# Attention weights divided on one engine: a fused attention and gated-MLP kernel on one core

## The chip, the cores and the metric

One core of a Trainium2 chip. The metric is device time in microseconds (us) of one execution, lower is better. The engines are named as in the profile: PE (TensorE), DVE (VectorE), ACT (ScalarE), POOL (GpSimd), SP (SyncE, which issues most DMAs).

## The reference

Three stages in float32 on batch 2, sequence 768:

```python
# 1. attention, 8 heads of 64; a key is kept if it is one of the first 8, or at most 95 back
scores = q @ k.T / 8 - slope[h] * dist        # NEG where not kept
a = exp(scores - max); a = a / (sum(a) + 1e-9)
x = a @ v                                     # heads side by side: (2, 768, 512)
# 2. gated value:  x = (sigmoid(causal conv5(x)) * (x @ w_val)) @ w_out
# 3. gated MLP:    h = relu(x @ w_in)         # 512 -> 1024
#                  out = (h * sigmoid(conv3(h))) @ w_out2   # 1024 -> 512
```

The weights come as float64 and are brought to float32 in the kernel.

## The kernel before, in words

*Attention.* `fast_attention` runs over 12 tiles of 128 queries (6 per batch). A tile sees its own 128 keys and the 128 of the tile before (the first 32 places of which are replaced by the global keys where needed, `first_keys`, L511), so it is 128x256 per head, 128x128 in the first tile of a batch. Per tile, in two halves of four heads: score products on PE (L461) into PSUM; on DVE bias and row minimum (L472, writes the tile `p`); on ACT the exponential in place with its row sum (L477); on POOL a guard of 1e-9 on the four sums (L488); on DVE their reciprocal (L491); then the **division**: each head's `p` is multiplied in place by its reciprocal, on DVE (L498) or on POOL (L501). PE transposes two heads at a time into one PSUM bank (L528); ACT or DVE copies them to `pts` (L532, L538); PE makes the output products (L553), and ACT or DVE copies the tile into `x` (L570, L576). There are 11 buffers for `p` and one PSUM bank for the transposes.

*Weights.* Each 128x512 unit of a float64 matrix comes by DMA as two words per value and passes ACT (L262), POOL (L264), and DVE twice (L269, L272); most are then split into a high and a low part (L234 on ACT, L236 on DVE) for three-term products (`mm3`, L243 to L245). `w_out @ w_in` is multiplied out first (L319).

*The rest.* Convolutions are chains of DVE steps (L671) opened on ACT or POOL (L666, L667); then values, hidden layer and projection for four chunks of the sequence.

*The order.* Every piece of work is handed to a `Plan` with its engine and an assumed duration. A piece may have several **ways** (engines): the planner picks the engine on which it would end first. It lays all work out by list scheduling in six passes, keeps the layout that ends first by its assumed durations, and issues every engine's instructions in that fixed order. Weight work has an earlier rank (`EARLY`). Before the change a division had two ways, with these assumed durations for `nk` keys:

```python
pl.add(
    "DVE", 0.13 + 0.00052 * nk, on_dve, [p[h], st], [("r", t, half)], [("p", t, h)],
    POOL=(0.1 + pool_us(nk), on_pool),          # pool_us(n) = 0.17 + 0.0013 * n
)
```

For 256 keys that is 0.263 us on DVE and 0.603 on POOL. The copies L532/L538 and L570/L576 have two ways as well, ACT and DVE.

Of the kernel before, what the change touches and what calls it, by code (L numbers as in the profile page):

```python
# [36 lines left out]
BIG = NEG * 2.0 ** NH * 1.01  # L37
QKSCALE = 1.0 / math.sqrt(D)
XPAIRS = 2
RAWS, MBUFS, HBUFS, Z2BUFS, PBUFS, PTBUFS, KQBUFS, VBUFS = 3, 2, 6, 3, 11, 4, 3, 4  # L40
EARLY = -5.0
LANDING = 2.4
# [40 lines left out]
class Plan:  # L83

    LAG = {"PE": 0.2, "ACT": 0.15, "DVE": 0.15, "POOL": 0.15, "SP": 0.0}
    START = {"DVE": 0.4, "ACT": 1.2, "SP": 0.3}
# [134 lines left out]
def pool_us(n):  # L223
    return 0.17 + 0.0013 * n
# [27 lines left out]
def to_f32(c, dst, raw, n, bufs, reads, token):  # L252
# [5 lines left out]
    def whole(): return high().bitcast(F32)  # L258
    def bits(): return dst().bitcast(I32)
# [3 lines left out]
    pl.add(  # L263
        "POOL", pool_us(n), lambda: nc.gpsimd.tensor_scalar(whole(), whole(), 0.0, 1.0, ALU.mult, ALU.mult),  # L264
        bufs, reads + [token], [tail],
# [143 lines left out]
def fast_attention(c, ap):  # L409

    nc, ident, pl = c.nc, c.ident, c.plan
# [29 lines left out]
    def held(d, ts):  # L441
        return [d[t] for t in ts if t in d]

    for t in range(nt):
        b, i = tiles[t]
        if t and i == 0:
            yield
        js = [t - 1, t] if i else [t]
        nk = len(js) * P
        st, p = sts.new(), {}  # L450
        load(t)
        for half in range(2):
            s = [c.ring["s"].new() for z in range(2)]

            def scores(half=half, s=s, js=js, t0=t):
                for pr in (2 * half, 2 * half + 1):
                    for n, j in enumerate(js):
                        for z in range(2):
                            hs = slice(z * D, (z + 1) * D)
                            out = s[z].t.rearrange("p (a w) -> p a w", w=WIN)[:, pr % 2, n * P : (n + 1) * P]  # L460
                            nc.tensor.matmul(out, keys(t0, pr, 1)[hs], keys(j, pr, 0)[hs], start=True, stop=True)  # L461

            pl.add(
                "PE", 0.43 * len(js), scores, s + held(kq, js), [("kq", j) for j in js], [("s", t, half)], mode="s"
            )
            for h in range(4 * half, 4 * half + 4):
                p[h] = pr_.new()

                def least(h=h, s=s, st=st, w=p[h], nk=nk, i=i):
                    sc = s[h % 2].t.rearrange("p (a w) -> p a w", w=WIN)[:, h // 2 % 2, :nk]  # L470
                    bias = c.B[:, h, :] if i else c.B0[h]
                    nc.vector.tensor_tensor_reduce(  # L472
                        w.t[:, :nk], sc, bias, -QKSCALE, 3.0e38, ALU.add, ALU.min, st.t[:, 0, h : h + 1]
                    )

                def grow(h=h, st=st, w=p[h], nk=nk):
                    nc.scalar.activation(  # L477
                        w.t[:, :nk], w.t[:, :nk], AF.Exp, bias=st.t[:, 0, h : h + 1], scale=-1.0,
                        accum_out=st.t[:, 1, h : h + 1],
                    )  # L480

                bias = ("B" if i else "B0", h)
                pl.add("DVE", dve_us(nk), least, [p[h], s[h % 2], st], [("s", t, half), bias], [("p", t, h)])
                pl.add("ACT", act_us(nk, True, True, True), grow, [p[h], st], [], [("p", t, h)])
            hs = slice(4 * half, 4 * half + 4)

            def guard(st=st, hs=hs):
                nc.gpsimd.tensor_scalar(st.t[:, 1, hs], st.t[:, 1, hs], 1.0e-9, 1.0, ALU.add, ALU.mult)  # L488

            def invert(st=st, hs=hs):  # L490
                nc.vector.reciprocal(st.t[:, 2, hs], st.t[:, 1, hs])  # L491

            four = [("p", t, h) for h in range(4 * half, 4 * half + 4)]
            pl.add("POOL", 0.12, guard, [st], four, [("r", t, half)])
            pl.add("DVE", 0.2, invert, [st], [], [("r", t, half)])
            for h in range(4 * half, 4 * half + 4):
                def on_dve(h=h, st=st, w=p[h], nk=nk):
                    nc.vector.tensor_scalar(w.t[:, :nk], w.t[:, :nk], st.t[:, 2, h : h + 1], None, ALU.mult)  # L498

                def on_pool(h=h, st=st, w=p[h], nk=nk):  # L500
                    nc.gpsimd.tensor_scalar(w.t[:, :nk], w.t[:, :nk], st.t[:, 2, h : h + 1], 1.0, ALU.mult, ALU.mult)  # L501

                pl.add(
                    "DVE", 0.13 + 0.00052 * nk, on_dve, [p[h], st], [("r", t, half)], [("p", t, h)],
                    POOL=(0.1 + pool_us(nk), on_pool),
                )

        def first_keys(t=t, i=i):
            r = (c.first[0] if t == 0 else kq[t].t)[:, :, 0, 0:GW]
            a, z = (gl, r) if i == 0 else (r, gl)  # L510
            nc.gpsimd.tensor_scalar(a, z, 1.0, 1.0, ALU.mult, ALU.mult)  # L511

        if i == 0:
            pl.add("POOL", 0.4, first_keys, held(kq, [t]), [("kq", t)], ["gl"])
        elif i < NT - 1:
            pl.add("POOL", 0.4, first_keys, held(kq, [t]), ["gl"], [("kq", t)])

        xp = c.ring["x"].new()
        pts = {}
        for pr in range(NPAIR):  # L520
            pt = c.ring["t"].new()
            pts[pr] = ptr.new()

            def turn(pr=pr, pt=pt, p=p, nw=len(js)):
                o = pt.t.rearrange("p (z n q) -> p z n q", z=2, n=2)
                for z in range(2):
                    for n in range(nw):
                        nc.tensor.transpose(o[:, z, n, :], p[2 * pr + z].t[:, n * P : (n + 1) * P], ident)  # L528

            def copy(pt=pt, w=pts[pr], nw=len(js)):  # L530
                o = pt.t.rearrange("p (z n q) -> p z n q", z=2, n=2)
                nc.scalar.activation(w.t[:, :, :nw, :], o[:, :, :nw, :], AF.Copy)  # L532

            two = [p[2 * pr], p[2 * pr + 1]]
            pl.add("PE", 0.218 * len(js), turn, [pt] + two, [("p", t, 2 * pr), ("p", t, 2 * pr + 1)], [("pt", t, pr)])
            def by_dve(pt=pt, w=pts[pr], nw=len(js)):
                o = pt.t.rearrange("p (z n q) -> p z n q", z=2, n=2)
                nc.vector.tensor_copy(w.t[:, :, :nw, :], o[:, :, :nw, :])  # L538

            pl.add(  # L540
                "ACT", act_us(2 * nk, False), copy, [pt, pts[pr]], [("pt", t, pr)], [("pts", t, pr)],
                DVE=(dve_us(2 * nk), by_dve),
            )

            if pr % XPAIRS < XPAIRS - 1:
                continue

            def output(prs=range(pr - XPAIRS + 1, pr + 1), pts=pts, xp=xp, js=js):
                o = xp.t.rearrange("p (a q) -> p a q", q=P)
                for pr in prs:  # L550
                    for n, j in enumerate(js):
                        for z in range(2):
                            nc.tensor.matmul(  # L553
                                o[z * D : (z + 1) * D, pr, :], vals(j, 2 * pr + z), pts[pr].t[:, z, n, :],
                                start=n == 0, stop=n == len(js) - 1,
                            )

            prs = range(pr - XPAIRS + 1, pr + 1)
            pl.add(
                "PE", 0.213 * len(js) * XPAIRS, output, [xp] + [pts[q] for q in prs] + held(vs, js),  # L560
                [("pts", t, q) for q in prs] + [("v", j) for j in js], [("xp", t, q) for q in prs], mode="x",
            )
        if 0 < i < NT - 1:
            pl.add(
                "SP", dma_us(64), lambda b=b, t=t: nc.sync.dma_start(vs[t].t[0:GW], c.v[b, 0:GW].rearrange("s (a h) d -> s a h d", a=2)),
                [vs[t]], [], [("v", t)], delay=LANDING,
            )
        pl.add(
            "ACT", act_us(512, False),
            lambda xp=xp, i=i: nc.scalar.activation(  # L570
                c.x[:, :, XP + i * P : XP + (i + 1) * P], xp.t.rearrange("p (a q) -> p a q", q=P), AF.Copy
            ),
            [xp], [("xp", t, pr) for pr in range(NPAIR)], [("x", i)] + (["d", "d0"] if t in (0, 1, 4) else []),
            DVE=(
                dve_us(512),
                lambda xp=xp, i=i: nc.vector.tensor_copy(  # L576
                    c.x[:, :, XP + i * P : XP + (i + 1) * P], xp.t.rearrange("p (a q) -> p a q", q=P)
                ),
            ),
        )  # L580
# [420 lines left out]
```

## Time and profile before

| | before |
|---|---|
| median of 3 runs | 289.19 us (288.85 to 289.6) |
| profiled execution | 289.12 us |
| its span (first to last instruction) | 286.9 us |
| PE, DVE, ACT, POOL busy | 270.1, 238.6, 187.2, 95.4 us |
| granted PE clock | 0.998 of full speed |
| divisions on DVE, on POOL | 46, 50 |

The time of a run is the span and some 2 us around it. A row of instructions is read as: line of the kernel, engine, operation, tile written <- tiles read, shapes and count; after the bar the busy time of the group, the mean in ns of one, and the idle time of the engine just before them with what ended it. PE's matmuls are pipelined and their ends are modelled, so a busy PE is not one at its peak. A row of windows has the stretch, its length, the busy time of each engine with the instructions that start in it, the granted clock, the share of the DMA engines and GB/s.

### The profile page before, as it was taken

To read this page: it belongs to the slowest core of one execution; us is meant where nothing else is said; L and a number is where in the kernel's file an instruction comes from. 1 tells how busy PE (TensorE), PEld (TensorE's weight loads), DVE (VectorE), ACT (ScalarE), POOL (GpSimd) and SP (SyncE) were. 2 spreads that over 40 slices of the span, in tenths; PEclk is the share of its full clock that TensorE was granted. 3 is DMA by queue.
4 is the path that set the end of the run, shared out by engine and by line. 5 is a ranking of instruction groups with operands and counts; after the bars stand their busy time and mean duration, and the time that the engine had idled before them with its cause. 6 is when DMAs were issued, how large, how long until landed. Compare 5 with 4: busy or idle time off the path is not lost.

```text
span 286.9 us, 5416 instructions
## 1 busy us (share of the span) xinstructions
PE 270.1 (94%) x1832; PEld 227.9 (79%) x1832; DVE 238.6 (83%) x607; ACT 187.2 (65%) x468; POOL 95.4 (33%) x208
## 2 busy tenths in 40 slices
PE   2689799999999999999999999999999999999993
PEld 2567556564557998999999999988999988899882
DVE  3899999999999999999899999999985654356600
ACT  2899798967677879775688554894464354445510
POOL 4555557445554405563443310320512000003000
PEclk9999999999999999999999999999999999999999
DMA  4985756645634111023510000010000011000112
GB/s 133 344 322 143 239 197 213 251 138 169 216 108 148 48 65 58 9 75 93 170 43 0 2 0 0 1 39 38 37 2 0 0 73 39 37 0 2 39 73 85
DMA packets 10276, 26.17 MB, mean 91 GB/s; under 512 B 1408, under 2 KB 2688, under 8 KB 10240
## 3 DMA queue, kind: packets, MB, share of 16 engines
q1 hardware_dynamic: 9440, 25.22, 26.3%
q10 hardware_dynamic: 800, 0.52, 0.6%
q8 instruction: 16, 0.26, 0.4%
q14 instruction: 20, 0.16, 0.2%
HBM read 22.59 MB, written 3.15 MB: 90 GB/s over the span
## 4 chain that ended last, share of the span: by engine, by line
PE 73%; DVE 15%; POOL 3%; issue 3%; ACT 3%; POOLq 1%; DVEq 0%; ACTq 0%
PE s L244 8%; PE s L245 8%; PE s L243 8%; PE f L243 7%; PE f L245 7%; PE f L244 7%; PE s L461 4%; PE x L553 4%; PE t L528 4%; DVE p L472 3%; DVE z L671 2%; PE t L243 2%; PE t L245 2%; PE x L245 2%; PE x L244 2%
## 5 line engine op out<-in xcount | busy, mean ns | idle before, releaser
L477 ACT ACTIVATE p<-p,st 128x256 f32<-128x256 f32 (+1 forms) x96 | 46.1, 483 | 8.0 <-DVE st L472 6.4
L671 DVE SCALAR_TENSOR_TENSOR z<-h,cw,z 128x384 f32<-128x384 f32 x64 | 39.9, 630 | 12.6 <-ACT z L666 10.9
L673 ACT ACTIVATE z<-z 128x384 f32<-128x384 f32 (+2 forms) x48 | 25.2, 524 | 26.2 <-DVE z L671 25.5
L671 DVE SCALAR_TENSOR_TENSOR z<-x,cw,z 128x400 f32<-128x400 f32 (+1 forms) x64 | 39.6, 643 | 0.2
L244 PE MATMUL s<-w,g 128*128 128x512 f32 (+1 forms) x104 | 39.2, 377 | 0.0
L245 PE MATMUL s<-w,g 128*128 128x512 f32 (+1 forms) x104 | 39.2, 377 | 0.0
L243 PE MATMUL s<-w,g 128*128 128x512 f32 (+1 forms) x104 | 39.1, 376 | 0.0
L501 POOL TENSOR_SCALAR p<-p,st 128x256 f32<-128x256 f32 (+1 forms) x50 | 32.5, 660 | 11.0 <-DVE st L491 8.7
L528 PEld LDWEIGHTS t<-ident,p 128*128 128x128 f32 x176 | 19.8, 141 | 16.6 <-issue 5.0
L528 PE MATMUL t<-ident,p 128*128 128x128 f32 x176 | 28.7, 282 | 4.1 <-ACT pts L532 2.1
L319 PE MATMUL f<-w,w 128*128 128x512 f32 x64 | 30.8, 602 | 0.0
L472 DVE CUSTOM_DVE_ANT_0 p<-s,B 128x256 f32<-128x256 f32 x80 | 30.5, 410 | 0.0
L243 PE MATMUL f<-gg,Wh 128*128 128x400 f32 (+1 forms) x80 | 27.7, 347 | 0.0
L245 PE MATMUL f<-gg,Wl 128*128 128x400 f32 (+1 forms) x80 | 27.0, 338 | 0.0
L244 PE MATMUL f<-gg,Wh 128*128 128x400 f32 (+1 forms) x80 | 27.0, 338 | 0.0
L461 PE MATMUL s<-kq 64*128 64x128 f32 x320 | 25.7, 292 | 0.8 <-DVE st L472 0.7
L461 PEld LDWEIGHTS s<-kq 64*128 64x128 f32 x320 | 21.5, 194 | 4.9 <-issue 2.6
L667 POOL TENSOR_SCALAR z<-h,cw 128x384 f32<-128x384 f32 x10 | 8.9, 887 | 45.9 <-DVE z L671 31.0
L264 POOL TENSOR_SCALAR raw<-raw 128x512 f32<-128x512 f32 x24 | 18.3, 764 | 16.7 <-ACT m L262 14.1
L236 DVE TENSOR_TENSOR g<-z,g 128x384 fp32r<-128x384 f32 x32 | 17.8, 562 | 5.9 <-ACT g L234 5.9
L245 PEld LDWEIGHTS s<-w,g 128*128 128x128 f32 x104 | 19.5, 188 | 3.8
L244 PEld LDWEIGHTS s<-w,g 128*128 128x128 f32 x104 | 19.6, 188 | 2.8
(117 smaller groups left out, 633.6 us busy)
## 6 DMA issues: line engine op xcount, KB each, us to landing
raw<-in_moe_w_out_dram SPq DMA_DIRECT2D x12, 512.0 KB, 3.4
kq<-in_kq_dram SPq DMA_DIRECT2D x11, 512.0 KB, 4.4
raw<-in_moe_w_in_dram SPq DMA_DIRECT2D x8, 512.0 KB, 5.3
v<-in_v_dram SPq DMA_DIRECT2D x11, 256.0 KB, 3.6
out_dram<-o SPq DMA_DIRECT2D x11, 256.0 KB, 2.0
raw<-in_moe_w_val_dram SPq DMA_DIRECT2D x4, 512.0 KB, 3.5
v<-in_v_dram SPq DMA_DIRECT2D x8, 64.0 KB, 2.8
x<-in_kq_dram ACTq DMA_DIRECT2D x1, 256.0 KB, 4.0
```

Of the source, the lines that this page charges most:

```text
L243: nc.tensor.matmul(out, lh, rh, start=first, stop=False)
L244: nc.tensor.matmul(out, lh, rl, start=False, stop=False)
L245: nc.tensor.matmul(out, ll, rh, start=False, stop=last)
L264: "POOL", pool_us(n), lambda: nc.gpsimd.tensor_scalar(whole(), whole(), 0.0, 1.0, ALU.mult, ALU.mult),
L319: nc.tensor.matmul(ps.t, big["wot"].t.bitcast(F32)[:, e, cs], big[wi].t.bitcast(F32)[:, e, :], start=e == 0, stop=e == 3)
L461: nc.tensor.matmul(out, keys(t0, pr, 1)[hs], keys(j, pr, 0)[hs], start=True, stop=True)
L472: nc.vector.tensor_tensor_reduce(w.t[:, :nk], sc, bias, -QKSCALE, 3.0e38, ALU.add, ALU.min, st.t[:, 0, h : h + 1])
L477: nc.scalar.activation(w.t[:, :nk], w.t[:, :nk], AF.Exp, bias=st.t[:, 0, h : h + 1], scale=-1.0, accum_out=st.t[:, 1, h : h + 1],)
L501: nc.gpsimd.tensor_scalar(w.t[:, :nk], w.t[:, :nk], st.t[:, 2, h : h + 1], 1.0, ALU.mult, ALU.mult)
L528: nc.tensor.transpose(o[:, z, n, :], p[2 * pr + z].t[:, n * P : (n + 1) * P], ident)
L671: nc.vector.scalar_tensor_tensor(z(), src(k), w()[:, k : k + 1], z(), ALU.mult, ALU.add)
L673: pl.add("ACT", act_us(n), lambda: nc.scalar.activation(z(), z(), AF.Tanh, scale=0.5), bufs, [], [token])
```

## The change

The division has one way only: POOL for every tile below `SHARED`, and `SHARED` is 12, the number of tiles. The duration assumed for POOL becomes 0.25 + 0.00094 * nk, which is 0.491 us for 256 keys and 0.370 for 128. Nothing else in the code differs; the planner lays out all work anew with it, the two-way copies included.

```diff
+SHARED = 12
...
-                pl.add(
-                    "DVE", 0.13 + 0.00052 * nk, on_dve, [p[h], st], [("r", t, half)], [("p", t, h)],
-                    POOL=(0.1 + pool_us(nk), on_pool),
-                )
+                e, us, fn = ("POOL", 0.25 + 0.00094 * nk, on_pool) if t < SHARED else ("DVE", 0.13 + 0.00052 * nk, on_dve)
+                pl.add(e, us, fn, [p[h], st], [("r", t, half)], [("p", t, h)])
```

## Rows read from the trace of the kernel before

**Rows 1.** The page: busy time, share of the span, instructions.

```profile
PE 270.1 (94%) x1832; PEld 227.9 (79%) x1832; DVE 238.6 (83%) x607; ACT 187.2 (65%) x468; POOL 95.4 (33%) x208
```

**Rows 2.** Windows: stretch, length, busy of PE, PEld, DVE, ACT, POOL.

```profile
9.00:20.00 11.00, 9.62 (x94) 7.79 (x95) 10.11 (x46) 9.76 (x36) 6.65 (x17) 1.00 0.94 331
20.00:40.00 20.00, 17.76 (x188) 13.80 (x188) 19.80 (x73) 17.06 (x54) 11.26 (x23) 1.00 0.69 218
40.00:91.00 51.00, 49.63 (x345) 29.26 (x343) 50.53 (x140) 39.56 (x109) 27.80 (x43) 1.00 0.54 180
91.00:130.00 39.00, 39.00 (x364) 36.16 (x364) 38.26 (x116) 31.73 (x91) 17.13 (x38) 1.00 0.15 47
```

**Rows 3.** The chain that ended last: start us, us, what.

```profile
20.46 1.09 PE s L461 x16
...
26.61 1.49 POOL p L501 x2
...
38.95 0.44 PE t L528 x4
39.39 1.72 PE f L319 x4
...
105.14 1.02 PE x L553 x16
```

**Rows 4.** Groups of PE, 9 to 91 us.

```profile
L319 PE MATMUL f<-w,w 128*128 128x512 f32 x64 | 30.8, 602 | 0.0
L461 PE MATMUL s<-kq 64*128 64x128 f32 x240 | 19.8, 294 | 0.8 <-DVE st L472 0.7
L528 PE MATMUL t<-ident,p 128*128 128x128 f32 x112 | 18.8, 284 | 4.1 <-ACT pts L532 2.1 <-DVE pts L538 2.0
L553 PE MATMUL x<-pts,v 128*64 128x128 f32 x160 | 10.7, 276 | 0.0
```

**Rows 5.** Groups of DVE, 9 to 91 us; then line 671: ns min/median/max.

```profile
L498 DVE TENSOR_SCALAR p<-p,st 128x256 f32<-128x256 f32 (+1 forms) x32 | 13.8, 454 | 0.0
L671 DVE SCALAR_TENSOR_TENSOR z<-x,cw,z 128x400 f32<-128x400 f32 x16 | 11.3, 709 | 0.0
...
L272 DVE SCALAR_TENSOR_TENSOR w<-w,raw 128x512 int32<-128x512 int32 x12 | 8.6, 719 | 0.2
...
L272 DVE SCALAR_TENSOR_TENSOR m<-m,raw 128x512 int32<-128x512 int32 x4 | 3.6, 889 | 0.1
...
L671 DVE SCALAR_TENSOR_TENSOR z<-x,cw,z x64: 567/620/1036, 46.5 to 211.6; 128x400 f32<-128x400 f32 x32, 128x368 f32<-128x368 f32 x32
```

**Rows 6.** Windows of line 498 alone: DVE busy (count).

```profile
20.00:40.00 20.00, 5.98 (x14) 1.00 0.69 218
40.00:91.00 51.00, 5.80 (x12) 1.00 0.54 180
91.00:130.00 39.00, 5.55 (x14) 1.00 0.15 47
```

**Rows 7.** Timeline, 39 to 44 us: start us, us, engine, line.

```profile
42.28 0.97 POOL L501 TENSOR_SCALAR p<-p,st 128x256 f32<-128x256 f32 x2 [0.93 <-DVE st L491]
43.22 0.68 POOL L264 TENSOR_SCALAR raw<-raw 128x512 f32<-128x512 f32 x1
...
39.03 0.34 DVE L498 TENSOR_SCALAR p<-p,st 128x256 f32<-128x256 f32 x1
39.30 0.68 DVE L269 SCALAR_TENSOR_TENSOR raw<-raw 128x512 int32<-128x512 int32 x1
...
43.16 0.88 DVE L498 TENSOR_SCALAR p<-p,st 128x256 f32<-128x256 f32 x1
```

**Rows 8.** Line 501: ns min/median/max, all; its groups, 20 to 40, 40 to 91 us.

```profile
L501 POOL TENSOR_SCALAR p<-p,st x50: 374/507/1310, 9.5 to 129.1; 128x256 f32<-128x256 f32 x42, 128x128 f32<-128x128 f32 x8
...
L501 POOL TENSOR_SCALAR p<-p,st 128x256 f32<-128x256 f32 x10 | 5.3, 543 | 2.5 <-DVE st L491 2.3
...
L501 POOL TENSOR_SCALAR p<-p,st 128x256 f32<-128x256 f32 (+1 forms) x20 | 15.3, 774 | 2.7 <-DVE st L491 2.7
```

## The prediction, made before the changed kernel was run

> **What bounds the kernel now.** I read the engines' totals first, then the stages by window, then the work of each engine inside the stage that the change touches, then the chain, then single instructions in order of time.
>
> Over the whole span TensorE is busy 94%, VectorE 83%, ScalarE 65%, GpSimd 33% [rows 1]. That average hides two halves. In the windows [rows 2] TensorE is busy 39.00 of 39 us from 91 to 130 us; before 91 us it is not full, and there VectorE is: 19.80 of 20 us in 20 to 40, 50.53 of 51 in 40 to 91. GpSimd has 11.26 of 20 and 27.80 of 51 in those two. GpSimd's last division starts at 129.1 us [rows 8], so nothing of the change is executed in the last half of the span.
>
> "Busy" of TensorE is stretched by waiting, so I work out what it really has to do from 9 to 91 us. The chain shows the pace when nothing holds it: 16 score products in 1.09 us, 4 transposes in 0.44, 4 weight products in 1.72, 16 output products in 1.02 [rows 3]. The counts of the window [rows 4], with 16 more of line 461 and 32 more of line 553 that read the first tile's copies, give 256 x 1.09/16 + 112 x 0.44/4 + 64 x 1.72/4 + 192 x 1.02/16 = 17.4 + 12.3 + 27.5 + 12.2 = 69.4 us of 82. So 12.6 us of TensorE time are lost before 91 us, and practically none after. That is the most this change can win, whatever it takes off VectorE. What TensorE waits for there is a mixture: copies of transposed weights and VectorE's scores [rows 4], and in the chain at 26.61 us GpSimd's own work, two divisions of 1.49 us together [rows 3]. GpSimd is already on the path in places.
>
> **The change, part by part.** Removed from VectorE: 46 multiplications of line 498. In 9 to 91 us they are 32 and 13.8 us busy, mean 454 ns [rows 5]; in 20 to 40 us 5.98 us, in 40 to 91 us 5.80, in 91 to 130 us 5.55 [rows 6]. One that nothing disturbs takes 0.34 us with the next instruction starting 0.27 us after it; one took 0.88 while GpSimd was at work [rows 7]. So what VectorE sheds before 91 us lies between 32 x 0.27 = 8.6 us and 13.8 us; I take 13.8, since the waits go with the instructions, but the lower value is kept for the slow case.
>
> Added to GpSimd: the same 46. Two that ran back to back undisturbed took 0.97 us, 0.48 each [rows 7]; the mean in 20 to 40 us was 543 ns, with VectorE in the way [rows 8]; the least, the median and the longest of all 50 are 374, 507 and 1310 ns [rows 8]. Cost before 91 us: between 32 x 0.48 = 15.4 us and 32 x 0.77 = 24.6 us (the mean in 40 to 91 us, where VectorE's convolutions ran beside them [rows 8]). GpSimd has 82 - 6.65 - 11.26 - 27.80 = 36 us free there [rows 2], so on the average the work fits.
>
> By stage it fits less well. In 20 to 40 us 14 divisions move: 11.26 + 14 x 0.48 = 18.0 of 20 us, and at 0.54 each 18.8. VectorE sheds 5.98 us there, but GpSimd lets the stage shrink by 1 to 2 us at most, unless the planner puts weight passes (line 264) later. I take 1 us. In 40 to 91 us 12 move: 27.80 + 12 x 0.48 to 0.77 = 33.6 to 37.0 of 51, no bound; VectorE sheds 5.80 us. TensorE's loss there is the rest of the 12.6 us after 9 to 20 us (the filling of the pipeline) and 20 to 40 us have had theirs; I put a third of it, about 4 us, in this stage and let half of that come back: 2 us. In 9 to 20 us a tile's four divisions stand in a row on GpSimd instead of being shared, which lengthens the first tiles by two divisions of the narrow kind, 2 x 0.37 [rows 8], less what VectorE is sooner free: 0. In 91 to 130 us TensorE is full, VectorE's 5.55 us are hidden behind it: 0. If that cover went (a transposition early in TensorE's fixed order, whose weights are late on GpSimd), each late division would cost its lateness directly; that is the slow rival.
>
> The wait that the change lengthens: in a group of four heads the last division now comes after four on one engine (4 x 0.48 = 1.9 us) where two and two took about 1 us. Queued behind it on GpSimd are the low-bits pass of a weight (line 264, for which VectorE's joins wait), the guard of the next four heads (line 488) and the first keys (line 511, for which TensorE's scores wait). Behind the late transposition on TensorE waits all of its order.
>
> The contention on VectorE. A division of VectorE from 43.16 us on took 0.88 us while GpSimd's pass from 43.22 took 0.68 [rows 7]: one of the two ran at full speed and the other waited for its end. With 32 more instructions on GpSimd, VectorE's instructions with two tensor operands meet more of them. They have lost little so far: 16 of line 671 with a mean of 709 ns against the line's median of 620 in the whole trace, 4 of line 272 with 889 against 12 with 719 [rows 5], so 1.4 + 0.7 = 2.1 us. GpSimd's load grows by 15.4 on 45.7 us, a third, in a shorter stage: I add 2 us of waits, with 0 and 32 x 0.48 = 15.4 us as ends. Net, VectorE is relieved by 11.8 us before 91 us. TensorE's gaps are 12.6 us in all, some of them the filling that VectorE does not cause, and GpSimd nearly fills 20 to 40 us: TensorE and GpSimd become what bounds, and the gain is the 3 us above and not 11.8.
>
> The Trainium skill, SBUF — State Buffer, "SBUF: two separate sides", says that VectorE and GpSimd share one pair of ports as an exclusive lock, held for a whole instruction, for VectorE's instructions with two inputs or in a two-port mode. The trace agrees (the 0.88 us above). By that rule every moved division exchanges a short hold by a longer one; the sum stays between the two ends named, and the rule's worst case is the slow rival.
>
> Copies, as the title of the change says, stay a choice between ScalarE and VectorE; the planner will hand VectorE some of those that ScalarE (17.06 of 20 us) [rows 2] does now. That costs VectorE part of its relief and TensorE nothing.
>
> Sum: 289.12 us (the profiled execution, 286.9 of it span; the median of the runs is 289.19) - 0 - 1 - 2 - 0 = 286.1 us.
>
> **Rivals.** *The gain is larger.* The planner sees a free VectorE, and the attention of the first batch and the weight products close most of TensorE's gaps: 6 to 8 of the 12.6 us, 281 to 283. For it: VectorE is the one saturated engine. Against: GpSimd at 18 of 20 us, and on the chain already.
>
> *The gain is eaten by GpSimd.* 24 divisions at 0.543 in 20 to 40 us with the other 6 us are 19.0, and the longer row of four delays the transpositions as much as the freed VectorE brings them forward: 288.1 to 290.
>
> *Slower: the moved division holds VectorE up.* One mechanism: each division on GpSimd makes a two-operand instruction of VectorE wait for its 0.48 us. Before 91 us 15.4 us of waits against 13.8 shed, +1.6; in 91 to 130 us 14 x 0.48 = 6.7 against 5.55, +1.2, and VectorE there is at 38.26 of 39 us [rows 2], so its lateness reaches TensorE: 291.9. It decides from the point where a moved division costs VectorE over 13.8/32 = 0.43 us. For it: the 0.88 us, and means of 774 ns on GpSimd in 40 to 91 us [rows 8], where the two meet most. Against: the 2.1 us are all that VectorE's other instructions have lost so far beside 30 divisions of GpSimd from 20 to 91 us [rows 8], 0.07 us for each.
>
> The Trainium skill, GPSIMD Engine Reference, "Engine selection", gives elementwise work to VectorE, and calls GpSimd about half as fast with two inputs and near full rate with one. This division has one tensor input, and 0.48 against 0.27 us [rows 7] is nearer to the half. What it does here as a mechanism is the second rival.
>
> **How the numbers follow.** Differences under 0.3% (0.9 us) can't be told from no change. Forecast, 284 to 287.5 us: 0.40. Larger gain, 281 to 284: 0.14. Eaten, 287.5 to 290: 0.19, of which 0.16 lie within 0.3%, the rest under it. Slower, 290 to 294: 0.27, a point of it within 0.3%. So faster 0.57, same 0.17, slower 0.26. The range from 282.3 to 291.9 leaves out the best of the larger gain and the worst of the slow case; the forecast's own is 284 to 287.5.
>
> **What would show it.** Right: no line 498 in attention; line 501 96 times, mean of 0.5 to 0.7 us; GpSimd over 17 of 20 us between 20 and 40; VectorE below 95% between 40 and 91; the weight products (line 319) done and TensorE without gaps 2 to 4 us sooner, and from there on an unchanged distance to the end. Wrong: VectorE's lines 671 and 272 with means up by 0.2 us or more; TensorE waiting for line 501 after 91 us; or TensorE's gaps before 91 us unchanged with VectorE idle, which would mean that VectorE's full load never was what held it.

## The result and the profile after

The changed kernel takes 292.89 us in the median of four runs (291.51 to 294.93) against 289.31 us before; the ratio is 1.0133, with a 95% interval from 1.0095 to 1.0172. It is slower by 1.3%, where 1.1% faster was forecast, and it lies above the range. The four times stand in two pairs, 291.5 to 291.6 and 294.2 to 294.9, so the median lies between two kinds of run. The profile first shown is of a run of 294.18 us (span 292.4); a run of 291.48 us is shown further down.

The page's busy times, and the windows of before [rows 2], for the changed kernel (stretch, length, busy of PE, PEld, DVE, ACT, POOL):

```profile
PE 272.2 (93%) x1832; PEld 229.2 (78%) x1832; DVE 226.4 (77%) x563; ACT 188.7 (65%) x473; POOL 119.5 (41%) x247
```

```profile
9.00:20.00 11.00, 9.34 (x66) 7.20 (x66) 7.58 (x35) 7.24 (x28) 7.88 (x20) 1.00 0.87 317
20.00:40.00 20.00, 18.01 (x191) 14.12 (x192) 17.91 (x62) 16.50 (x52) 16.09 (x30) 1.00 0.52 164
40.00:91.00 51.00, 48.65 (x347) 28.58 (x344) 47.50 (x130) 39.89 (x112) 37.94 (x60) 1.00 0.60 195
91.00:130.00 39.00, 36.85 (x342) 33.71 (x343) 36.84 (x107) 32.49 (x94) 26.58 (x48) 1.00 0.28 87
```

The reader is to see two things. VectorE is relieved as intended (17.91 of 20 us, 47.50 of 51). But TensorE, which had 39.00 of 39 us and 364 matmuls between 91 and 130 us before, now has 36.85 and 342: it waits in the stage where the forecast let the change cost nothing. Some lines move by one: the division on GpSimd is line 502 here (501 before), the guard 489, the reciprocal 492, the transposition 527, ScalarE's copy of it 531, VectorE's 537, the convolution step 670, the score products 462.

The divisions and VectorE's two-operand instructions [rows 5, 8], now by group, the first from 91 to 130 us, the others from 9 to 91; then two groups of the kernel before, the divisions from 91 to 130 us and its line 269 (270 now) from 9 to 91:

```profile
L502 POOL TENSOR_SCALAR p<-p,st 128x256 f32<-128x256 f32 x27 | 19.0, 719 | 2.0 <-DVE st L492 0.9 <-PE f L246 0.7 <-PE f L245 0.4
...
L502 POOL TENSOR_SCALAR p<-p,st 128x256 f32<-128x256 f32 (+1 forms) x66 | 41.7, 645 | 6.8 <-DVE st L492 4.4 <-PE s L462 1.6 <-PE x L552 0.4
...
L270 DVE SCALAR_TENSOR_TENSOR raw<-raw 128x512 int32<-128x512 int32 x16 | 12.3, 769 | 0.6 <-POOL raw L265 0.6
L670 DVE SCALAR_TENSOR_TENSOR z<-x,cw,z 128x400 f32<-128x400 f32 x16 | 11.7, 753 | 0.0
...
L501 POOL TENSOR_SCALAR p<-p,st 128x256 f32<-128x256 f32 x14 | 9.0, 655 | 4.9 <-DVE st L491 3.1 <-PE f L244 0.8 <-PE f L245 0.7
L269 DVE SCALAR_TENSOR_TENSOR raw<-raw 128x512 int32<-128x512 int32 x16 | 10.9, 681 | 0.0
```

A division on GpSimd takes 0.65 to 0.72 us in the mean, not the 0.48 of two that ran undisturbed nor the 0.49 that the planner now assumes. The median of all 96 is 480 ns: about half take what the planner assumes, and a tail up to 1490 ns makes the mean. The 14 that GpSimd had in this stage before took 655 in the mean. VectorE's lines lost only a little more than before: line 670 753 ns against 709.

**Where TensorE's time went.** As in the prediction I count the matmuls that start in a stretch and multiply by the undisturbed pace of each kind (score 0.068 us, transposition 0.109, weight product 0.430, output 0.064; of the three-term products 0.182 with 400 columns, 0.169 with 368, 0.233 with 512, 0.114 with 256). The sum is 261.2 us in every kernel; the stretch less that work is lost. Each row is one profiled execution, within 0.5 us of its median but for the run of 294.18, e3 (291.79) and e4 (287.84). The idle products (below) are not counted as work, so their time counts as lost.

| kernel | median us | ratio to before [95%] | lost to 20 us | 20-40 | 40-91 | 91-130 | 130-150 |
|---|---|---|---|---|---|---|---|
| before | 289.31 | | 12.0 | 4.6 | 3.9 | 0.4 | 0.2 |
| changed (run of 294.18) | 292.89 | 1.0133 [1.0095, 1.0172] | 14.1 | 4.4 | 4.2 | 3.2 | 0.6 |
| changed again, e14 (291.48) | | | 12.2 | 3.9 | 4.0 | 3.2 | 0.5 |
| e1 old order, all on GpSimd | 291.79 | 1.0091 [1.0059, 1.0124] | 12.1 | 4.5 | 4.5 | 2.0 | 1.2 |
| e13 old order, 46 on ScalarE | 293.03 | 1.0110 [1.0083, 1.0138] | 12.7 | 7.0 | 2.7 | 2.9 | -0.1 |
| e2 new order, half on VectorE | 297.00 | 1.0268 [1.0235, 1.0300] | 12.2 | 5.7 | 5.0 | 5.4 | 0.7 |
| e3 changed + idle products | 291.02 | 1.0047 [1.0028, 1.0065] | 11.8 | 3.5 | 5.1 | 3.3 | 0.6 |
| e4 before + idle products | 289.93 | 1.0009 [0.9981, 1.0037] | 11.1 | 4.5 | 3.6 | 0.8 | 0.0 |
| e5 e3, short divisions | 285.28 | 0.9848 [0.9820, 0.9875] | 11.8 | 2.7 | 2.5 | 0.8 | 0.0 |
| e9 e3, short convolution steps | 284.76 | 0.9843 [0.9814, 0.9872] | 11.8 | 3.7 | 1.7 | 0.2 | 0.1 |
| e6 e3, measured duration assumed | 289.77 | 1.0006 [0.9985, 1.0028] | 11.8 | 4.9 | 3.9 | 0.8 | 1.3 |
| e7 idle products, first batch on GpSimd alone | 291.22 | 1.0065 [1.0038, 1.0093] | 11.0 | 4.4 | 6.2 | 2.0 | 0.3 |
| e8 idle products, second batch on GpSimd alone | 292.39 | 1.0100 [1.0069, 1.0131] | 11.7 | 3.1 | 5.3 | 1.1 | 3.4 |
| e10 two ways, measured durations + idle products | 288.74 | 0.9969 [0.9944, 0.9994] | 11.8 | 2.2 | 3.6 | 0.3 | 3.7 |
| e11 three ways + idle products | 287.36 | 0.9938 [0.9916, 0.9961] | 11.2 | 3.6 | 3.7 | 1.0 | 0.2 |
| e12 three ways | 288.71 | 0.9972 [0.9948, 0.9997] | 12.7 | 4.0 | 3.8 | 0.9 | 0.2 |

In the run of 294.18 us the 5.4 us more that are lost up to 150 us are 2.1 in the filling, 2.8 between 91 and 130 us, and 0.5 elsewhere; the span is 5.5 longer. In the run of 291.48 us the filling loses only 0.2 more and the stage from 91 to 130 us loses the same 2.8. So there are two causes.

**First cause, between 91 and 130 us.** TensorE is idle there three times, each time before a transposition; two in its timeline (in brackets the idle time and what ended it):

```profile
101.13 0.66 PE L527 MATMUL t<-ident,p 128*128 128x128 f32 x4 [0.57 <-ACT pts L531]
...
123.89 0.63 PE L527 MATMUL t<-ident,p 128*128 128x128 f32 x4 [0.47 <-ACT pts L531]
```

The third and longest, 1.10 us before 127.81, in the chain of waits of the changed kernel (start us, us, what):

```profile
120.72 3.33 POOL p L502 x3
...
124.39 0.56 POOL z L666
...
125.03 0.20 POOL st L489
...
125.26 0.18 DVE st L492
125.44 0.52 DVE z L670
...
125.98 0.74 DVE z L670
126.72 0.33 DVE p L473
...
127.06 0.61 DVE pts L537
...
127.81 0.63 PE t L527 x4
```

It reads from above: four divisions in a row are late; behind them on GpSimd, and behind the opening of a convolution (666), the guard of the next four heads (line 489) is late; VectorE's reciprocal (492) waits for it; behind the reciprocal in VectorE's fixed order stand two convolution steps, a score and the copy of the last transposition (537); and TensorE cannot transpose into its one bank before that copy. The wait is put down to VectorE; its origin is GpSimd. The transposition does not wait for its own two divisions: they had ended 6.0 us before it. With divisions and transpositions paired by their order, the 13 groups of transpositions of this stage (two heads each) begin 0.38 to 9.9 us after their divisions end, 5.35 in the median. So what a late division holds up is what stands behind it on GpSimd.

The other two waits end with a copy by ScalarE. At 101.13 us no division is in the chain: the copy stood behind two exponentials and the opening of a convolution on ScalarE. At 123.89 us it stood behind an exponential; VectorE's score for that one ran from 122.16 to 122.56, after the four subtractions shown next (the profile names a division that ended 0.02 us later). So 1.10 of the 2.15 us of idle time are traced to late divisions.

Why the four are late shows the timeline of GpSimd and VectorE there (start us, us, engine, line):

```profile
119.87 0.87 POOL L502 TENSOR_SCALAR p<-p,st 128x256 f32<-128x256 f32 x1 [0.38 <-PE f L245]
120.72 1.12 POOL L502 TENSOR_SCALAR p<-p,st 128x256 f32<-128x256 f32 x1
121.82 0.75 POOL L502 TENSOR_SCALAR p<-p,st 128x256 f32<-128x256 f32 x1
122.56 1.49 POOL L502 TENSOR_SCALAR p<-p,st 128x256 f32<-128x256 f32 x1
...
119.94 0.54 DVE L237 TENSOR_TENSOR gx<-x,gx 128x368 fp32r<-128x368 f32 x1
120.39 0.73 DVE L237 TENSOR_TENSOR gx<-x,gx 128x368 fp32r<-128x368 f32 x1
121.05 0.53 DVE L237 TENSOR_TENSOR gx<-x,gx 128x368 fp32r<-128x368 f32 x1
121.50 0.73 DVE L237 TENSOR_TENSOR gx<-x,gx 128x368 fp32r<-128x368 f32 x1
...
122.50 0.68 DVE L273 SCALAR_TENSOR_TENSOR m<-m,raw 128x512 int32<-128x512 int32 x1
123.10 0.68 DVE L237 TENSOR_TENSOR w<-m,w 128x512 fp32r<-128x512 f32 x1
...
125.26 0.18 DVE L492 RECIPROCAL st<-st 128x4 f32<-128x4 f32 x1 [1.48 <-POOL st L489]
```

Four divisions take 4.17 us (119.87 to 124.05) where 4 x 0.48 = 1.9 would do. Each ends 0.26 to 0.35 us after the end of an instruction of VectorE with two tensor operands (those that end at 120.48, 121.58, 122.23 and 123.78 us). The second and the fourth see two such instructions through, and take 1.12 and 1.49 us; VectorE's second and fourth subtraction take 0.73 us where the others take 0.54 and 0.53. The two engines get in by turns, and GpSimd misses two turns. The Trainium skill, SBUF — State Buffer, "SBUF: two separate sides", calls this an exclusive lock on shared ports, held for an instruction; the trace agrees (the 0.26 to 0.35 us).

**Second cause, in some executions: the pace of TensorE at the start.** The chain of the run of 294.18 us from 12 us on, and its window from 14 to 22 us:

```profile
15.72 0.66 PE t L527 x2
16.38 1.05 PE x L552 x8
17.43 2.01 PE s L462 x16
19.45 0.62 PE t L527 x2
20.06 1.92 PE s L462 x16
21.98 0.60 PE t L527 x4
```

```profile
14.00:22.00 8.00, 6.94 (x47) 5.25 (x48) 5.93 (x24) 4.08 (x14) 4.14 (x10) 1.00 0.56 211
```

The same order of TensorE in the run of 291.48 us, timeline (a merged row's time includes the drain of its last matmul), and its window:

```profile
15.55 0.66 PE L552 MATMUL x<-pts,x 128*64 128x128 f32 x8
16.14 1.16 PE L462 MATMUL s<-kq 64*128 64x128 f32 x16
17.23 0.44 PE L527 MATMUL t<-ident,p 128*128 128x128 f32 x2
17.60 1.16 PE L462 MATMUL s<-kq 64*128 64x128 f32 x16
```

```profile
14.00:22.00 8.00, 6.17 (x66) 4.64 (x66) 7.63 (x32) 6.63 (x23) 6.54 (x14) 1.00 0.80 286
```

16 score products take 2.01 us in one and 1.09 (16.14 to 17.23) in the other: about half the pace, as the lower of TensorE's two levels would give, 1.2 in place of 2.4 GHz, until 21.98 us. The granted clock stands at 1.00 in both windows, so that column does not show it; the level is read from the pace alone. Before it TensorE had done 32 scores from 9 to 13 us and then three pairs of transpositions with waits of 0.61 us between them, in both runs. The runs part at the second pair: it takes 0.66 us from 14.46 us in the one and 0.41 from 14.19 in the other. The Trainium skill, TensorE: Matmul & The Clock Gate, Part 1, describes a gate that lets half of the pulses through until the array has been busy; the half pace agrees with it.

### The profile page after: what moved, and what is told of

It is laid out like the page before. It is cut to its first block, busy times and chain, and to the rows that moved or that the text cites. A ratio compares the mean times of both kernels' runs of the same rounds, so it can differ in the third digit from the quotient of the medians.

```text
span 292.4 us, 5474 instructions
## 1 busy us (share of the span) xinstructions
PE 272.2 (93%) x1832; PEld 229.2 (78%) x1832; DVE 226.4 (77%) x563; ACT 188.7 (65%) x473; POOL 119.5 (41%) x247
## 4 chain that ended last, share of the span: by engine, by line
PE 74%; DVE 10%; ACT 5%; issue 4%; POOL 3%; SPq 1%; DMA 1%; ACTq 0%; DVEq 0%; POOLq 0%
PE s L245 8%; PE s L246 8%; PE s L244 8%; PE s L462 7%; PE f L244 7%; PE f L245 7%; PE f L246 6%; PE t L527 6%; PE x L552 4%; DVE z L670 3%; ACT p L478 2%; PE f L320 2%; PE x L246 2%; PE t L246 2%; DVE raw L270 2%
## 5 line engine op out<-in xcount | busy, mean ns | idle before, releaser
L502 POOL TENSOR_SCALAR p<-p,st 128x256 f32<-128x256 f32 (+1 forms) x96 | 62.4, 664 | 9.2 <-DVE st L492 5.3
L670 DVE SCALAR_TENSOR_TENSOR z<-x,cw,z 128x400 f32<-128x400 f32 (+1 forms) x64 | 40.7, 662 | 0.5 <-ACT z L665 0.3
L527 PE MATMUL t<-ident,p 128*128 128x128 f32 x176 | 29.5, 288 | 7.7 <-ACT pts L531 3.5
L462 PEld LDWEIGHTS s<-kq 64*128 64x128 f32 x320 | 22.4, 208 | 5.2 <-issue 4.5
L666 POOL TENSOR_SCALAR z<-h,cw 128x384 f32<-128x384 f32 x7 | 5.6, 801 | 47.4 <-DVE z L670 30.7
L531 ACT ACTIVATE pts<-t 128x512 f32<-128x512 f32 (+1 forms) x34 | 19.4, 570 | 6.9 <-PE t L527 6.8
```

The lines of the kernel that those rows point to most:

```text
L670: nc.vector.scalar_tensor_tensor(z(), src(k), w()[:, k : k + 1], z(), ALU.mult, ALU.add)
```

## Experiments

My theory after the profile: late divisions on GpSimd make TensorE wait in the second batch (through the queue behind them, as the chain above shows), and the lower pace adds to it in some executions. Rivals: the planner's new order as such; VectorE and GpSimd keeping each other waiting, as opposed to any engine that gets 46 more pieces.

**e1: the old order, the engine alone changed.**

```diff
-                pl.add(
+                w = pl.add(
                     "DVE", 0.13 + 0.00052 * nk, on_dve, [p[h], st], [("r", t, half)], [("p", t, h)],
                     POOL=(0.1 + pool_us(nk), on_pool),
                 )
+                w.issued = "POOL"
...
-            w.ways[w.eng][1]()
+            w.ways[getattr(w, "issued", w.eng)][1]()
```

> The layout of the kernel before is kept to the last instruction; only the 46 divisions that it gave to VectorE are issued on GpSimd, at the same places of the order. If late divisions cost the time (GpSimd's divisions are stretched by VectorE's two-operand instructions and TensorE waits): 292 to 295 us, with TensorE's loss between 91 and 130 us up from 0.4 by 2 us or more. If the new layout costs it (the planner's order, not the engine): 288 to 290. If the lower pace of TensorE at the start costs it: the order of the filling is the old one, so 16 score products at 14 us take 1.1 us again and the time is at most 290.5.

291.79 us: slower by 0.9% with not one other instruction moved. TensorE loses 2.0 us between 91 and 130 us, where it lost 0.4, and 1.0 more behind that; the filling is as before. That is just under the 292 expected, and the stage loses some 1.5 us more, not 2. The new order is not needed for a loss. Here too TensorE's longest wait between 91 and 150 us, 0.87 us before 138.57, goes back to divisions, this time through the weight pass behind them on GpSimd (264) and VectorE's join (269), at the end of whose row stands the copy (539):

```profile
131.43 2.20 POOL p L501 x3
133.63 0.62 POOL raw L264
...
134.30 0.68 DVE raw L269
...
137.83 0.61 DVE pts L539
...
138.57 0.63 PE t L529 x4
```

**e2: the new order, half of the divisions on VectorE.**

```diff
+                if h % 2:
+                    w.instead = on_dve
...
-            w.ways[w.eng][1]()
+            getattr(w, "instead", w.ways[w.eng][1])()
```

> The layout of the changed kernel is kept; every second head's division is issued on VectorE at its place in that order. If late divisions on GpSimd cost the time: 289 to 290.5, since GpSimd has half of them. If the layout costs it: 292 or more still.

297.00 us, a miss: taking half of the divisions from GpSimd made it 4.1 us slower than the changed kernel. By the sentence on record this is the case of the layout, and against late divisions on GpSimd. But VectorE, on which the new order counts without divisions, is full in this run: 19.97 of 20 us, 49.94 of 51 and 38.70 of 39. So the run brings a load of its own, and does not tell the theories apart as I had thought.

**e3, e4: idle products for the pace at the start.** Both keep every order; only TensorE gets six products of the identity into an unused bank behind the first tile's scores.

```diff
+            extra = [c.ring["f"].new()] if t == 0 and half == 1 else []
...
+                for f in extra:
+                    for _ in range(6):
+                        nc.tensor.matmul(f.t[:, 0:P], ident, ident, start=True, stop=True)
```

> The changed kernel, same layout, with six idle products of the identity put into TensorE's empty time behind the first tile's scores (7 to 9 us). If TensorE's lower pace until 21.9 us is a part of the loss: 16 scores at 17 us take 1.1 us instead of 2.0, and the time falls by 1.5 to 3 us to 290 to 291.4, with less spread between runs. If it is a mere sign of waiting: within 0.9 us of 292.9.

> The same six idle products in the kernel before. It reaches the full pace at 14 us by itself: the lower pace as a cause gives 0 to 1.5 us less (287.8 to 289.3); otherwise no change or up to 0.4 more.

The changed kernel falls by 1.87 us to 291.02, and its twelve times lie between 290.75 and 292.0. The timeline of e3 shows the full pace from the start of the second tile:

```profile
10.74 0.39 PE L462 MATMUL s<-x,kq 64*128 64x128 f32 x4
10.96 0.39 PE L462 MATMUL s<-kq 64*128 64x128 f32 x4
...
15.17 1.16 PE L462 MATMUL s<-kq 64*128 64x128 f32 x16
```

The kernel before gains nothing measurable (1.0009, interval across 1; 287.84 to 291.54). Its times spread with the idle products as well, so the spread of that kernel has another source, which I did not look for. So the pace is a part of the changed kernel's loss, half of the median's 3.6 us. The idle products take away the slower kind of run; against the faster pair (291.5) they gain 0.5 us. The other part, with 3.3 us lost between 91 and 130 us, is still there.

**e5: shorter divisions.** On e3, the same order.

```diff
-                    nc.gpsimd.tensor_scalar(w.t[:, :nk], w.t[:, :nk], st.t[:, 2, h : h + 1], 1.0, ALU.mult, ALU.mult)
+                    nc.gpsimd.tensor_scalar(w.t[:, :64], w.t[:, :64], st.t[:, 2, h : h + 1], 1.0, ALU.mult, ALU.mult)
```

> The changed kernel with the six idle products (291.02 us) and the same layout; GpSimd divides only the first 64 columns of each head and leaves the rest undivided. If it is the length of GpSimd's divisions that makes TensorE wait: 288.0 to 289.7 us, with TensorE's loss between 91 and 150 us (3.9 with the whole divisions) under 1.5. If the layout as such costs the time: 290.5 to 291.5.

**e9: shorter convolution steps on VectorE.** On e3, the same order.

```diff
-            nc.vector.scalar_tensor_tensor(z(), src(k), w()[:, k : k + 1], z(), ALU.mult, ALU.add)
+            q = slice(0, 32)
+            nc.vector.scalar_tensor_tensor(z()[:, q], src(k)[:, q], w()[:, k : k + 1], z()[:, q], ALU.mult, ALU.add)
```

> The changed kernel with the idle products (291.02 us), same layout; VectorE's convolution steps (line 670 of the changed kernel) work on 32 columns instead of 368 to 400, the rest is left out. GpSimd's divisions are untouched. If they are long because VectorE's two-operand instructions keep them waiting: their mean falls from 673 ns to 600 or less, most of it between 91 and 130 us, and the time to 286.5 to 289. If they are long by themselves: mean over 640, and the time moves only by what VectorE's own work held up, at most 1.5 us.

The groups of divisions from 91 to 130 us in e3, e5 and e9:

```profile
L510 POOL TENSOR_SCALAR p<-p,st 128x256 f32<-128x256 f32 x25 | 17.5, 715 | 2.4 <-DVE st L500 0.9 <-PE f L245 0.8 <-PE f L246 0.7
```

```profile
L510 POOL TENSOR_SCALAR p<-p,st 128x64 f32<-128x64 f32 x28 | 12.7, 472 | 3.3 <-DVE st L500 1.7 <-PE f L245 0.9 <-PE f L246 0.7
```

```profile
L510 POOL TENSOR_SCALAR p<-p,st 128x256 f32<-128x256 f32 x28 | 16.1, 592 | 2.3 <-PE f L245 0.7 <-PE f L246 0.6 <-DVE st L500 0.6
```

With divisions of 472 ns, close to the 0.49 that the planner assumes, the order fits: 285.28 us, 5.7 us less, and 0.8 us lost between 91 and 130 us. That is below the 288.0 expected: the shorter divisions also win 3.5 us between 20 and 91 us, where e3 loses about what the kernel before does (8.6 against 8.5). So e5 takes away more than the change had added. e9 leaves the divisions alone and still shortens them from 715 to 592 ns there, 673 to 600 over all: VectorE's two-operand instructions do stretch them, by 123 ns in that stage. But 284.76 us, below the 286.5 expected, is more than that can give; VectorE itself had much less to do (30.71 of 39 us against 36.76), so e9 does not price the contention alone.

**e13: the 46 on ScalarE in the old order**, as e1 with ScalarE in GpSimd's place:

```diff
+                def on_act(h=h, st=st, w=p[h], nk=nk):
+                    nc.scalar.activation(w.t[:, :nk], w.t[:, :nk], AF.Copy, scale=st.t[:, 2, h : h + 1])
...
+                w.instead = {"DVE": on_act}
```

> The layout of the kernel before, to the last instruction; the 46 divisions that it gave to VectorE are issued on ScalarE, at the same places of the order, instead of on GpSimd (291.79 us). A division takes some 0.4 to 0.5 us on either. If it is the meeting of GpSimd and VectorE that makes the moved divisions late: 288 to 290.3, since ScalarE has no such waits. If any in-order engine that is not planned for them is as bad: 291 to 294; ScalarE is the fuller of the two (66 of 82 us against 46 before 91 us).

293.03 us, inside the range for any in-order engine and against the theory that the meeting of the two engines is what counts. The group of its divisions from 9 to 91 us:

```profile
L504 ACT ACTIVATE p<-p,st 128x256 f32<-128x256 f32 (+1 forms) x32 | 15.0, 482 | 0.0
```

These divisions run without stretching (482 ns), and TensorE still loses 2.9 us between 91 and 130 us, and 2.4 more than before between 20 and 40, where ScalarE is now busy 20.00 of 20 us. 46 more pieces on an engine whose queue was not laid out for them cost time on either of the two; a loss of this size needs no contention. How much of GpSimd's own loss contention makes is not shown: ScalarE was the fuller engine, and e1's divisions took 579 ns in the mean between 91 and 130 us, less than the changed kernel's 719.

**e6: the planner is told the measured duration**, all on GpSimd, with the idle products: `0.16 + 0.00195 * nk` (0.66 us for 256 keys) instead of `0.25 + 0.00094 * nk`.

> The same with whole divisions, all on GpSimd, but the planner is told 0.66 us for 256 keys and 0.41 for 128, about what the trace shows, instead of 0.49 and 0.37. If transpositions stand too early in TensorE's order because the planner takes a division for shorter than it is: 289 to 290.3. If GpSimd simply cannot give the divisions in time, or the planner loses elsewhere what it wins here: 290.7 to 293.

289.77 us, 1.25 less than e3, and 0.8 us lost between 91 and 130 us instead of 3.3. Its row of that stage has TensorE at 38.95 us:

```profile
91.00:130.00 39.00, 38.95 (x359) 35.79 (x356) 37.98 (x107) 31.24 (x90) 26.64 (x50) 1.00 0.23 72
```

GpSimd has as much to do as in e3 (26.64 against 25.70 us), so it can give the divisions in time. What in the new layout does it is not shown. It is not that the transpositions stand further behind their divisions: in this stage they begin 3.1 us after them in the median, 5.7 in e3. A part of the gain is lost again behind it (1.3 us from 130 to 150 us against 0.6). All in all that is as fast as before the change, and no faster.

**e7, e8: one batch each on GpSimd alone**, the other on either engine, with the idle products.

> With the idle products; divisions of the first batch on GpSimd alone, those of the second on either engine with the assumed durations of before. If the loss left after the idle products is made in the second batch (91 to 150 us): 288.5 to 290.2. If in the first: 290.5 to 292.

> The other way round: first batch on either engine, second on GpSimd alone. If the loss left is made in the second batch: 290.5 to 292; if in the first: 288.5 to 290.2.

291.22 and 292.39 us (ratios 1.0065 and 1.0100). Inconclusive: e7 lies in and e8 above the 290.5 to 292 expected where the batch left on GpSimd alone makes the loss, so each accuses its own batch. e7 loses 6.2 us between 40 and 91 us and, with two engines for the second batch, still 2.0 between 91 and 130; e8 loses 1.1 there and 3.4 between 130 and 150. The planner lays everything anew for each, and the new order's own losses are as large as what was to be told apart.

**e10, e11, e12: a better version.** Durations near the measured ones for two ways, then ScalarE as a third, with and without idle products:

```diff
+                pl.add(
+                    "DVE", 0.24 + 0.00052 * nk, on_dve, [p[h], st], [("r", t, half)], [("p", t, h)],
+                    POOL=(0.16 + 0.00195 * nk, on_pool), ACT=(act_us(nk, True, True), on_act),
+                )
```

> Divisions on either engine as before the change, with the idle products, but with assumed durations near the measured ones (0.373 us on VectorE, 0.66 on GpSimd for 256 keys). If the planner's too short durations cost the kernel before as well: 287 to 289; if two engines leave enough slack anyway: 289 to 290.5.

> The same with ScalarE as a third way (0.398 us assumed for 256 keys). ScalarE has 66 of 82 us before 91 us and shows no waits for the other two. If the contention of VectorE and GpSimd is what the divisions suffer from: 285.5 to 288.5. If ScalarE, which makes the exponentials, becomes late itself: 289.5 to 292.

> Three ways without the idle products: within 1 us of the run with them, if this order of the filling reaches the full pace by itself as the kernel before does; 2 us more if it stays slow until 22 us as the changed kernel does.

Two ways: 288.74 us (0.9969, 0.9944 to 0.9994), in the range for too short durations before. Three ways with idle products: 287.36 us, ratio 0.9938 (0.9916 to 0.9961), the fastest whole kernel here; 32 divisions on VectorE, 37 on GpSimd, 27 on ScalarE. It lies in the range expected if contention is what the divisions suffer from, but a third engine also gives more room, and the run does not part the two. Without the idle products 288.71 (0.9972), 1.35 us more, between the two cases on record; its twelve times spread from 287.42 to 290.03, and in the profiled one (289.01) TensorE reaches the full pace only at 18.00 us, as the second cause would have it.

**e14: the changed kernel again**, for the second profile shown above.

> The changed kernel once more, for a second profile. Its four times stand in two pairs, 291.5 and 294.5. If the pairs differ by how long TensorE keeps the lower pace at the start: a run near 291.5 has 16 score products in 1.1 us from 17 us on, one near 294.5 in 2.0 us until about 22.

291.48 us, with the score products at the full pace from 16.14 us on, as expected of the faster pair. That is one profile of either kind. What decides between the two in one execution stays open: the orders are the same, and the waits before differ by little.

## Why the prediction was wrong

- *What bounds the kernel.* Right in that TensorE's gaps before 91 us were the only gain to be had, and that GpSimd was on the path already. Wrong in what followed from "practically none after": the stage where TensorE was full had no reserve, and it lost 2.8 us.
- *91 to 130 us, the step that failed.* "TensorE is full, VectorE's 5.55 us are hidden behind it: 0" measured +2.8 us, in both profiles of the changed kernel. The case named behind it, a transposition whose own weights are late, is not what came: the transpositions there began 0.38 us or more after their divisions. The divisions were longer than the order assumed (0.72 us in the mean for 0.49), and late was what stood behind them on GpSimd: the guard in the changed kernel, the weight pass in e1. Through VectorE's fixed order the copy that empties the transpositions' one bank came late. The paragraph on the wait that the change lengthens lists both, and the sum has no term for either. e1, e5 and e6 bear it out: moving the 46 alone brings a loss, divisions of 0.47 us leave 0.8 us of it, and so does telling the planner 0.66. Traced to the divisions are 1.10 of the 2.15 us of idle time; for the rest it stays argued from these runs.
- *20 to 91 us, forecast -3.* In the execution with the full pace (e14) the loss falls from 4.6 to 3.9 us between 20 and 40 and stays at 4.0 against 3.9 behind that: a gain of 0.6 instead of 3. VectorE was idle there for 1.0 of 20 and 3.2 of 51 us, so this is nearly the last sign of being wrong: its full load was not what held TensorE. The limit that I set for 20 to 40 us held: GpSimd is at 19.02 of 20 us there in e14, and 16.09 in the first profile.
- *The filling, forecast 0.* 0.2 us in e14 and +2.1 in the run of 294.18 us. TensorE's two paces were visible before too (16 scores in 2.08 us at 4.88 us, 1.09 later), and I took the later one for the whole stage.
- *VectorE's relief and the slow rival.* The relief came (47.50 of 51 us). The price of contention on VectorE is near what I took: between 9 and 91 us line 670 lost 16 x 0.044 and line 270 16 x 0.088 us more than before, 2.1 us, as against 2 forecast; with the groups that fell (line 273 on `m` from 889 to 721 ns) all two-operand groups together lost 1.5. That is 0.05 to 0.07 us for a moved division, far from the 0.43 at which the slow rival decides. So the sign of that rival came true by another mechanism: GpSimd was held up far more than VectorE.
- *The price of a division.* I kept 0.48 to 0.77; 0.645 and 0.719 were measured. It was inside, but the median was 480 ns and the tail made the lateness. I summed only engine loads with it and never compared it with the 0.49 in the planner's list, which stands in the diff.
- *The sum.* 286.1 forecast. In the spans, e14 is 286.9 - 0.6 + 2.8 + 0.2 + 0.3 (130 to 150 us) + 0.1 (behind that) = 289.7; its time is 291.48 us, inside the range. The lower pace adds 2.7 and takes the median of two and two runs out of it; that the range held for the faster pair is luck, since the stages came out otherwise.

## What to carry to other kernels

Where a planner writes a fixed order, a piece's assumed duration is part of the change: compare it with the duration in place, stretched by its neighbours, before counting loads. A stage that is full by its bound engine is not safe ground for a zero; ask what the bound engine's next instruction needs, in which queues that stands, and what the change puts ahead of it there. Moving work into an order that was not laid out for it cost time on each of the three engines tried here (e1, e13, e2).

## What was not expected of the hardware

- Beside six two-operand instructions of VectorE four divisions of GpSimd took 4.17 us instead of 1.9, each ending 0.26 to 0.35 us after one of them; convolution steps shortened on VectorE made GpSimd's divisions 123 ns shorter.
- In one program TensorE goes over to the full pace at 14.2 us in one execution and at 22 us in another, 2.7 us apart in the end, with the granted clock at 1.00 in both; with six idle products in the gap before the second tile none of twelve runs was of the slower kind.
